# Linear attention and two MoE layers on one core: banks by kind, a head pair moved forward, Strassen's second product in the first MoE's last pair

## The chip, the cores and the metric

The kernel runs on one core of one Trainium2 chip. The metric is the device time of a whole execution in microseconds. TensorE (PE in the profile) multiplies matrices into PSUM, whose eight banks hold 512 fp32 values per partition each; its weight loads are listed as PEld. VectorE (DVE) and ScalarE (ACT) do elementwise work, SyncE (SP) issues every DMA.

## The reference

```python
kv = np.einsum('bhsd,bhse->bhde', k, v)            # 8 batches, 8 heads, 576 positions, 64 wide
out = np.einsum('bhsd,bhde->bhse', q, kv)
x = out / np.sqrt(np.mean(out * out, -1, keepdims=True) + 1e-06) * g_norm   # then (4608, 512)
r = np.maximum(x @ w_in, 0.0);  x = (s * (r * r) + b) @ w_out               # first MoE, d_ff 2048
h = x @ w2_in;  out = (h * (1.0 / (1.0 + np.exp(-1.702 * h)))) @ w2_out     # second MoE, d_ff 2048
```

## The kernel before, in words

The 4608 tokens are 9 blocks (j) of 512. Every product of fp32 values is made of three matmuls in fp32r: each operand is split into a high part (ACT copies to fp32r) and a low part (DVE subtracts), and high x high, high x low and low x high are added in PSUM. The weights arrive as 64-bit words and are converted on ACT and DVE (w_low, w_top, w_sum: lines L138 to L152).

Blocks 0 to 2 of the first MoE and block 8 of the second are done plainly: `mlp_h` makes one of 16 hidden parts f (12 matmuls into one bank h, L447), `mlp_act` applies the activation and gives the bank back, `mlp_g` splits, and `mlp_o` adds 12 matmuls into the four banks of the block's output (L490). The other blocks go in pairs. `first_products` makes x @ w_in by Strassen's scheme in Winograd's form: seven products a to g for each of 8 pairs of hidden parts (L533), with sums on DVE. For the second product, the first MoE's pairs (3, 4), (5, 6), (7, 8) use `second_plain` (16 parts x 2 blocks x 12 matmuls, L490), and the second MoE's pairs use `second_products` (seven products of 4 groups of 12 matmuls, L661; `go_sum`, `go_hi`, `go_lo` make its operands, L626, L635, L640). Strassen's weight operands (A11, S1 and so on) lie in DRAM.

Attention for block j and head pair p is a row of seven steps: `att_product` (o_ps, L345), square, low, `att_mean` (ms, L373), `att_root`, `att_newton` (L387 to L389, the last reader of both banks) and `att_split`. Products k^T v (kv) of the next batches come two head pairs at a time (L316, L320); ACT copies them out (L324, L325).

All order is written out by hand. `at(slot, function, ...)` puts a step at a slot; one slot is 12 matmuls of PE. The steps are sorted by slot and then issued, so every engine and the DMA queue of SP works in that order. Tiles are taken from lists of numbered places: 43 big and 20 middle ones in SBUF and 8 PSUM banks. A place that is given back goes to the end of its list, and the next taker gets the first; a taker waits on the chip until the last reader is done.

`START` holds the slots of the four head pairs of block 0: kv product; attention product, square and low; mean and root; newton; split.

Of the kernel before, what the change touches and what calls it, by code (L numbers as in the profile page):

```python
# [26 lines left out]
START = [(-61, -60, -54, -52, -45), (-59, -54, -53, -47, -42), (-54, -48, -48, -43, -41), (-50, -49, -46, -40, -36)]  # L27
# [12 lines left out]
LAG = 2  # L40
G1_ACT = (0, 0, 0, 1.5, 0.2, 1.6, 1.6)
# [20 lines left out]
def kernel(ctx: ExitStack, tc: tile.TileContext, qT, kv_h, kvt, cst,  # L62
# [32 lines left out]

    def psum(name):
        return new(bank, [P, T], F32, name)
# [23 lines left out]
    raws, vals, W = {}, {}, {}  # L121
# [49 lines left out]
    wod = [dp.tile([P, 2, 512], F32, name=f"wod{f}") for f in range(NF)]  # L171
    wsd = [[dp.tile([P, len(OPS), 512], F32, name=f"wsd{m}_{i}") for i in range(NF // 2)] for m in range(2)]
    wo2 = [dp.tile([P, NF // 2, 512], F32, name=f"wo2{name}") for name in OPS]

    def op_place(m, i, which, name):
        return wo2[OPS.index(name)][:, i, :] if which else wsd[m][i][:, OPS.index(name), :]
# [6 lines left out]
    def wo_store(f):  # L183
        nc.sync.dma_start(out=wod[f], in_=W[0, f, 1].bitcast(F32))

    def wo_load(m, f):
        w = W[m, f, 1] = new4(F32R, "w")
        if m == 0:
            nc.sync.dma_start(out=w.bitcast(F32), in_=wod[f])
        else:  # L190
            for a, name in enumerate(OP_PAIRS[1][f % 2]):
                nc.sync.dma_start(out=w[:, a, :].bitcast(F32), in_=op_place(m, f // 2, 1, name))

    def a_store(f):
        w = W[0, f, 0]
        for c, name in enumerate(OP_PAIRS[0][f % 2]):
            nc.sync.dma_start(
                out=op_place(0, f // 2, 0, name).rearrange("p (h c) -> p h c", h=2),
                in_=w[:, :, c * 256:(c + 1) * 256].bitcast(F32),
            )  # L200

    def w_join(f):
        w = W[0, f, 0]
        q = vals[0, f, 0] = new2(U32, "ca")
        dve.tensor_add(out=q.bitcast(F32), in0=w[:, 0, :].bitcast(F32), in1=w[:, 1, :].bitcast(F32))

# [43 lines left out]
    def wi_load(m, f):  # L250
        t = W[m, f, 0] = new4(F32R, "w")
        for a, name in enumerate(OP_PAIRS[0][f % 2]):
            nc.sync.dma_start(out=t[:, a, :].bitcast(F32), in_=op_place(m, f // 2, 0, name))

    def w_part(m, f, which, h, c):
        w = W[m, f, which]
        if m == 0:
            return w[:, h, c * P:(c + 1) * P]
        return w[:, c // 2, h * 256 + c % 2 * P:h * 256 + (c % 2 + 1) * P]
# [179 lines left out]
    def mlp_h(m, j, f):  # L439
# [9 lines left out]
        if m or j == NPLAIN - 1:  # L449
            drop(W.pop((m, f, 0)))  # L450
        if f == NF - 1:
# [41 lines left out]
    def wo_done(m, f):  # L493
        drop(W.pop((m, f, 1)))

# [93 lines left out]

    def g2_scale(q, n):  # L590
# [56 lines left out]
    def go_load(k, n):  # L647
        t = wl["o", k, n] = new4(F32R, "wl")
        nc.sync.dma_start(out=t.bitcast(F32), in_=wo2[OPS.index(PRODUCTS[k][0])][:, 2 * n:2 * n + 2, :])
# [40 lines left out]
    def g2_store(j, k, d):  # L690
        n, half = {3: (1, 2), 4: (0, 0), 5: (0, 2), 6: (1, 0)}[k]
        o_store(1, j + n, half + d, so.pop(("st", k, d)))
# [31 lines left out]
    def first_products(m, base, shift):  # L724
        for i in range(NF // 2):
# [7 lines left out]
            if i % 2 and m == 0:  # L733
                for n, (q, fn) in enumerate((("22", AF.Relu), ("21", AF.Relu), ("22", AF.Square), ("21", AF.Square),
                                             ("12", AF.Relu), ("11", AF.Square), ("12", AF.Square))):
                    at(slot + 1.4 + 0.45 * n, r_act, q, i // 2, fn)
            elif i % 2:
                at(slot + 3.1, t_sums, i // 2)
        return base + 28 + shift

    def second_plain(j, base):
        for f in range(NF):
            at(base + 2 * f - LEAD, wo_load, 0, f)
# [13 lines left out]
    def second_products(j, base):  # L757
        for k in range(len(PRODUCTS)):
            for n in range(4):
                slot = base + 4 * k + n  # L760
                at(slot, g2_product, k, n)
                at(slot - LEAD, go_load, k, n)
# [3 lines left out]
            for d in range(2):  # L766
                at(slot + 0.6 + 0.5 * d, g2_sum, j, k, d)
                if k > 2:
                    at(slot + 2.6, g2_store, j, k, d)
# [212 lines left out]
```

## Time and profile before

| | us |
|---|---|
| median of 3 runs (lowest, highest) | 1580.91 (1580.14, 1582.62) |
| the profiled execution | 1580.11 |
| its span, first to last instruction | 1578.3 |
| mean granted clock of TensorE | 0.998 |

A profile lists every instruction of one execution with its engine, start and length. A wait of an engine is put down to the instruction whose semaphore came last. "h <- DVE y L389" reads: the product h was waiting for the DVE operation of line 389. The granted clock is the share of 2.4 GHz; 0.5 is 1.2 GHz.

### The profile page before, as it was taken

The numbers are of one execution on the slowest core, as the hardware profiler recorded it, in microseconds if no ns is written. First come the engines' busy times: TensorE is split into PE (matmuls) and PEld (weight loads), VectorE is DVE, ScalarE is ACT, GpSimd is POOL, SyncE is SP. The second block draws the span as 40 slices with busy tenths as digits, with TensorE's granted clock in tenths as the row PEclk, the third lists the DMA queues.
The fourth block names the chain that finished last, engine by engine and source line by source line (L and its number), as shares of the span: only waits on it lengthen the run. The fifth ranks groups of instructions, "written<-read, shape, count | busy, mean of one in ns | idle before, by whom it ended". The sixth has DMA issues, their size and how long they took to land.

```text
span 1578.3 us, 19674 instructions
## 1 busy us (share of the span) xinstructions
PE 1552.8 (98%) x6904; PEld 1274.9 (81%) x6904; DVE 1095.9 (69%) x1583; ACT 861.0 (55%) x1283; POOL 2.4 (0%) x12
## 2 busy tenths in 40 slices
PE   7998999999999999999999999999999999999999
PEld 5777888788788877888888888888888888888887
DVE  5987356776789578856672679777967896688422
ACT  5987566655898379944783225423532452334222
POOL 0000000000000000000000000000000000000000
PEclk9999999999999999999999999999999999999999
DMA  9863646658987798859970866885788577745780
GB/s 323 250 204 113 233 138 230 224 189 308 341 278 280 243 377 277 306 181 358 333 295 0 301 239 236 273 299 200 269 284 303 200 250 262 263 149 205 230 296 27
DMA packets 171298, 385.36 MB, mean 244 GB/s; under 512 B 21312, under 2 KB 56768, under 8 KB 171200
## 3 DMA queue, kind: packets, MB, share of 16 engines
q1 hardware_dynamic: 171200, 384.11, 70.1%
q8 instruction: 55, 0.90, 0.2%
q14 instruction: 43, 0.35, 0.1%
HBM read 292.95 MB, written 91.10 MB: 243 GB/s over the span
## 4 chain that ended last, share of the span: by engine, by line
PE 76%; ACT 2%; DVE 2%; DMA 1%; issue 1%; DVEq 0%; ACTq 0%
PE o L490 21%; PE o L661 19%; PE d L533 9%; PE a L533 9%; PE h L447 4%; PE b L533 4%; PE f L533 4%; PE c L533 4%; ACT r L588 1%; DMA wsd<-op 1%; PE o_ps L345 0%; PE ms L373 0%; DMA wl<-wsd 0%; DVE y L387 0%; DVE y L388 0%
## 5 line engine op out<-in xcount | busy, mean ns | idle before, releaser
L490 PE MATMUL o<-gh,w 128*128 128x512 f32 x1280 | 409.7, 393 | 0.2
L490 PEld LDWEIGHTS o<-gh,w 128*128 128x128 f32 x1280 | 240.9, 188 | 52.0 <-DVE w L167 0.8
L661 PE MATMUL o<-gh,wl 128*128 128x512 f32 x896 | 276.7, 389 | 0.0
L490 PE MATMUL o<-gl,w 128*128 128x512 f32 x640 | 250.1, 391 | 0.3 <-DVE gl L480 0.2
L661 PEld LDWEIGHTS o<-gh,wl 128*128 128x128 f32 x896 | 168.3, 188 | 34.8
L447 PE MATMUL h<-xh,w 128*128 128x512 f32 x512 | 174.6, 403 | 8.8 <-DVE y L389 4.9
L661 PE MATMUL o<-gl,wl 128*128 128x512 f32 x448 | 174.5, 389 | 0.0
L533 PE MATMUL d<-xh,wl 128*128 128x512 f32 x448 | 157.5, 392 | 0.2
L533 PE MATMUL a<-xh,wl 128*128 128x512 f32 x448 | 157.7, 393 | 0.0
L490 PEld LDWEIGHTS o<-gl,w 128*128 128x128 f32 x640 | 120.7, 189 | 27.2 <-DVE gl L480 1.3
L447 PEld LDWEIGHTS h<-xh,w 128*128 128x128 f32 x512 | 96.9, 189 | 32.5 <-issue 5.6
L549 ACT ACTIVATE c<-a 128x512 f32<-128x512 f32 x56 | 33.3, 595 | 157.1 <-PE a L533 151.4
L447 PE MATMUL h<-xl,w 128*128 128x512 f32 x256 | 100.8, 394 | 0.4 <-DVE xl L409 0.4
L533 PEld LDWEIGHTS d<-xh,wl 128*128 128x128 f32 x448 | 84.2, 188 | 18.5 <-DVE r L559 1.0
L533 PEld LDWEIGHTS a<-xh,wl 128*128 128x128 f32 x448 | 84.1, 188 | 17.8 <-issue 0.2
L661 PEld LDWEIGHTS o<-gl,wl 128*128 128x128 f32 x448 | 84.1, 188 | 17.4
L604 DVE TENSOR_TENSOR gl<-r,gh 128x512 fp32r<-128x512 f32 x96 | 65.2, 687 | 46.4 <-ACT gh L599 45.0
L635 ACT ACTIVATE gh<-t 128x1024 fp32r<-128x1024 f32 x48 | 51.0, 1062 | 71.8 <-DVE t L626 71.6
L533 PE MATMUL a<-xl,wl 128*128 128x512 f32 x224 | 87.3, 390 | 0.0
L533 PE MATMUL d<-xl,wl 128*128 128x512 f32 x224 | 87.3, 390 | 0.0
L588 ACT ACTIVATE r<-r 128x1024 f32<-128x1024 f32 x84 | 84.9, 1047 | 0.0
L570 ACT ACTIVATE t<-a 128x512 f32<-128x512 f32 x32 | 19.1, 598 | 117.4 <-PE a L533 105.8
(118 smaller groups left out, 2719.4 us busy)
## 6 DMA issues: line engine op xcount, KB each, us to landing
wl<-wsd SPq DMA_DIRECT2D x168, 512.0 KB, 7.1
wl<-wo2S SPq DMA_DIRECT2D x64, 512.0 KB, 5.1
wsd<-op SPq DMA_DIRECT2D x96, 256.0 KB, 4.0
w<-wod SPq DMA_DIRECT2D x48, 512.0 KB, 6.1
wl<-wo2A SPq DMA_DIRECT2D x48, 512.0 KB, 3.7
raw<-in_w_in SPq DMA_DIRECT2D x32, 512.0 KB, 8.1
kv_in<-in_kv SPq DMA_DIRECT2D x32, 512.0 KB, 5.6
raw<-in_w_out SPq DMA_DIRECT2D x32, 512.0 KB, 7.6
```

Of the source, the lines that this page charges most:

```text
L447: pe.matmul(h, lhsT=a, rhs=b, start=(n == 0), stop=(n == 3 * NP - 1))
L490: pe.matmul(acc[m, j][c], lhsT=a, rhs=x, start=(f == 0 and n == 0), stop=(f == NF - 1 and n == 2))
L533: pe.matmul(o, lhsT=a, rhs=b, start=(first and n == 0), stop=(n == 5), skip_group_check=not first)
L549: act.activation(st["c1"], st[0], AF.Copy)
L570: act.activation(t, h, AF.Sigmoid, scale=1.702)
L588: act.activation(R[q, n], R[q, n], fn)
L604: dve.tensor_sub(out=gl, in0=R[q, i][:, half, :], in1=gh.bitcast(F32))
L635: act.activation(hi, src, AF.Copy)
L661: pe.matmul(so[k, d], lhsT=a, rhs=b, start=(first and n == 0 and i == 0 and e == 0), stop=(n == 3 and i == 1 and e == 2), skip_group_check ...
```

## The change

PSUM: a bank now remembers the kind of its last user. Attention's o_ps and ms are kind 1, h and kv kind 2, all others 0. A taker of kind 1 or 2 gets the first free bank that its own kind had last, if there is one, and the first of the list if not. `START` moves the third head pair forward, and the other times a little. The pair (7, 8) of the first MoE uses `second_products`; so W_out's operands of the first MoE are kept in DRAM in Strassen's form too (`part_store`, `w_rejoin`, `s_sums` and the rest during the second product of pair (3, 4)), and `part_load` reads a plain weight in two DMAs from there. That pair's activations get an order of their own. The conversions of the second MoE's weights go by a list, `CONV_AT`, of slots; before, there was one each 9.5 slots from 100, W_in and W_out in turn. The first stage of the second MoE gets its operands from `x_sums` and `x_splits`. In block 0 the even hidden parts are split as in blocks 1 and 2.

```diff
-START = [(-61, -60, -54, -52, -45), (-59, -54, -53, -47, -42), (-54, -48, -48, -43, -41), (-50, -49, -46, -40, -36)]
+START = [(-61, -60, -54, -52, -45), (-59, -54, -53, -47, -43), (-54, -51, -49, -45, -42.5), (-50, -48.9, -46, -41, -40.6)]
+SECOND = 7
+CONV_AT = ((97, 4), (156, 4), (188, 4), (221, 1), (232, 1), (250, 1), (278, 1))
...
+    last = {}
     def psum(name):
+        kind = {"o_ps": 1, "ms": 1, "h": 2, "kv": 2}.get(name, 0)
+        own = [n for n in bank.free if last.get(n) == kind]
+        if kind and own:
+            bank.free.remove(own[0])
+            bank.free.insert(0, own[0])
+        last[bank.free[0]] = kind
         return new(bank, [P, T], F32, name)
...
+    def part_load(m, f, which):
+        w = W[m, f, which] = new4(F32R, "w")
+        for a, name in enumerate(OP_PAIRS[which][f % 2]):
+            nc.sync.dma_start(out=w[:, a, :].bitcast(F32), in_=op_place(m, f // 2, which, name))
+        loaded.add((m, f, which))
...
+    def w_rejoin(f):
+        w = W[0, f, 1]
+        q = vals[0, f, 1] = new2(U32, "ca")
+        dve.tensor_add(
+            out=q.bitcast(F32).rearrange("p (a c) -> p a c", a=2),
+            in0=w[:, :, 0:256].bitcast(F32), in1=w[:, :, 256:512].bitcast(F32),
+        )
...
-        if m == 0 and j == 0:
+        if m == 0 and j == 0 and f % 2:
             act.activation(r, r, AF.Identity, scale=s_col, bias=b_col)
             act.activation(gh, r, AF.Copy)
         elif m == 0:
...
+            elif m == 0:
+                at(slot - 1.2, r_act, "11", i // 2, AF.Square)
+                at(slot - 0.7, g2_scale, "11", i // 2)
+                for n, q in enumerate(("22", "12", "21")):
+                    at(slot + 0.6 + n, r_relu2, q, i // 2)
+                    at(slot + 1.2 + n, g2_scale, q, i // 2)
+                at(slot + 3.0, t_sums, i // 2)
...
     for j in range(NPLAIN, NB, 2):
         firsts[0, j] = base
-        seconds[0, j] = first_products(0, base, LAG if j == NPLAIN else 0)
-        base = second_plain(j, seconds[0, j])
+        both = j >= SECOND
+        seconds[0, j] = first_products(0, base, LAG if j == NPLAIN else 0, both)
+        base = second_products(0, j, seconds[0, j]) if both else second_plain(j, seconds[0, j])
...
-    x_operands(1, 0, seconds[0, NB - 2] + 5, 2.3)
-    for j in range(0, NB - 3, 2):
-        x_sums(j + 2, firsts[1, j] + 4, 2)
-        x_splits(j + 2, seconds[1, j] + 5, 3.1)
+    for j, k in [(0, (0, NB - 2))] + [(j + 2, (1, j)) for j in range(0, NB - 3, 2)]:
+        x_sums(j, firsts[k] + 4 if j else seconds[0, NPLAIN] + 24, 2)
+        x_splits(j, seconds[k] + 5, 3.1)
...
+    for i in range(NF // 2):
+        slot = seconds[0, NPLAIN] + 4 * i
+        at(slot - 0.6, w_rejoin, 2 * i)
+        at(slot + 1.4, w_rejoin, 2 * i + 1)
+        at(slot + 2.2, s_sums, 0, i, 1)
+        for k in (2, 3):
+            at(slot + k + 1, op_hi, 0, i, 1, k)
+            at(slot + k + 1.7, op_lo, 0, i, 1, k)
+            at(slot + k + 4, op_store, 0, i, 1, k)
+        at(slot + 5, op_done, 0, i, 1)
```

## Rows read from the trace of the kernel before

**Rows 1.** The page: busy us, share of the span, instructions of each engine

```profile
PE 1552.8 (98%) x6904; PEld 1274.9 (81%) x6904; DVE 1095.9 (69%) x1583; ACT 861.0 (55%) x1283; POOL 2.4 (0%) x12
```

**Rows 2.** Chain that ended last: start us, length us, engine and line

```profile
791.02 87.04 PE o L490 x384
...
1106.57 76.16 PE o L661 x336
```

**Rows 3.** Waits of PE: us in total, times, longest

```profile
PE h L447 <- DVE y L389: 4.9, 1, 4.9
PE o_ps L345 <- DVE y L389: 3.1, 1, 3.1
...
PE h L447 <- ACT r L459: 1.1, 1, 1.1
```

**Rows 4.** Busy time by stage: first token block, then blocks two and three

```profile
27.00:153.70 126.70, 113.86 (x531) 90.37 (x529) 109.75 (x192) 107.86 (x193) 0.00 (x0) 0.97 0.65 204
153.70:358.60 204.90, 202.77 (x932) 167.86 (x931) 118.72 (x195) 125.27 (x201) 0.00 (x0) 1.00 0.61 206
```

**Rows 5.** Timeline of the start, by engine: DVE, PE, ACT (start, length us)

```profile
17.38 0.75 DVE L389 SCALAR_TENSOR_TENSOR y<-o_ps,g_col,y 128x512 f32<-128x512 f32 x1
...
26.97 0.58 PE L447 MATMUL h<-xh,w 128*128 128x512 f32 x1
...
32.88 0.25 ACT L324 ACTIVATE kvs<-kv 64x128 f32<-64x128 f32 x1
33.15 0.27 ACT L325 ACTIVATE kvs<-kv 64x128 f32<-64x128 f32 x1
...
38.94 0.60 ACT L459 ACTIVATE r<-h 128x512 f32<-128x512 f32 x1
...
44.76 0.59 ACT L459 ACTIVATE r<-h 128x512 f32<-128x512 f32 x1
```

**Rows 6.** Timeline of PE and ACT around a kv product of block two

```profile
165.71 1.95 PE L316 MATMUL kv<-kv_in 128*128 128x128 f32 x16
...
167.73 0.58 PE L447 MATMUL h<-xh,w 128*128 128x512 f32 x1
168.12 0.27 ACT L324 ACTIVATE kvs<-kv 64x128 f32<-64x128 f32 x1 [2.55 <-PE kv L320]
...
168.40 0.27 ACT L325 ACTIVATE kvs<-kv 64x128 f32<-64x128 f32 x1
```

**Rows 7.** Timeline at the start of the last block

```profile
1487.20 0.39 PE L447 MATMUL h<-xh,w 128*128 128x512 f32 x1
...
1490.12 0.60 ACT L462 ACTIVATE r<-h 128x512 f32<-128x512 f32 x1 [19.08 <-PE h L447]
...
1490.75 0.69 DVE L463 TENSOR_TENSOR r<-h,r 128x512 f32<-128x512 f32 x1 [2.66 <-ACT r L462]
```

**Rows 8.** Busy time in a second_products stage: PE, PEld, DVE, ACT

```profile
1117.30:1128.20 10.90, 10.90 (x50) 9.04 (x49) 10.37 (x10) 6.95 (x8) 0.00 (x0) 1.00 0.61 197
1128.20:1139.00 10.80, 10.80 (x49) 8.97 (x48) 10.80 (x11) 5.21 (x5) 0.00 (x0) 1.00 0.72 239
```

**Rows 9.** Timeline of DVE and PE in the same stage

```profile
1117.76 1.23 DVE L640 TENSOR_TENSOR gl<-r,gh 128x1024 fp32r<-128x1024 f32 x1 [1.72 <-ACT gh L635]
...
1141.90 1.21 DVE L640 TENSOR_TENSOR gl<-t,gh 128x1024 fp32r<-128x1024 f32 x1
...
1144.71 0.39 PE L661 MATMUL o<-gl,wl 128*128 128x512 f32 x1
```

**Rows 10.** DVE timeline of a weight conversion, and groups of two lines

```profile
62.37 0.42 DVE L145 TENSOR_SCALAR cu<-cu 128x512 f32<-128x512 f32 x1
...
64.63 0.68 DVE L167 TENSOR_TENSOR w<-ca,w 128x512 fp32r<-128x512 f32 x1
...
L230 DVE TENSOR_TENSOR op<-ca,op 128x512 fp32r<-128x512 f32 x32 | 21.8, 683 | 0.8 <-ACT op L225 0.8
...
L588 ACT ACTIVATE r<-r 128x1024 f32<-128x1024 f32 x84 | 84.9, 1047 | 0.0
```

**Rows 11.** Busy time and granted clock (0.83) around a stall of PE

```profile
80.00:90.00 10.00, 7.70 (x35) 6.22 (x36) 9.51 (x18) 7.21 (x13) 0.00 (x0) 0.83 0.58 196
```

More of the change, by code (lines that the diff above doesn't have):

```diff
@@ L248, in op_load @@
         nc.sync.dma_start(out=t[:, 0:n, :].bitcast(F32), in_=wsd[m][i][:, 2 * k:2 * k + n, :])
[L250 to L253, printed above, removed]
     def w_part(m, f, which, h, c):
         w = W[m, f, which]
-        if m == 0:
-            return w[:, h, c * P:(c + 1) * P]
-        return w[:, c // 2, h * 256 + c % 2 * P:h * 256 + (c % 2 + 1) * P]
+        if (m, f, which) in loaded:
+            return w[:, c // 2, h * 256 + c % 2 * P:h * 256 + (c % 2 + 1) * P]
+        return w[:, h, c * P:(c + 1) * P]
     kvin, kvs, qin, xT, done = {}, {}, {}, {}, set()
@@ L732, in first_products @@
                     at(slot - LEAD, op_load, m, i, k // 2)
-            if i % 2 and m == 0:
+            if i % 2 == 0:
+                continue
+            slot += 1.2
+            if m == 0 and not both:
                 for n, (q, fn) in enumerate((("22", AF.Relu), ("21", AF.Relu), ("22", AF.Square), ("21", AF.Square),
                                              ("12", AF.Relu), ("11", AF.Square), ("12", AF.Square))):
-                    at(slot + 1.4 + 0.45 * n, r_act, q, i // 2, fn)
-            elif i % 2:
-                at(slot + 3.1, t_sums, i // 2)
+                    at(slot + 0.2 + 0.45 * n, r_act, q, i // 2, fn)
+            elif m == 0:
[5 more added lines that the diff above has]
+                at(slot + 3.0, t_sums, i // 2)
+            else:
+                at(slot + 1.9, t_sums, i // 2)
         return base + 28 + shift
@@ L755, in second_plain, with second_products @@
         return base + 32
-    def second_products(j, base):
+    def second_products(m, j, base):
         for k in range(len(PRODUCTS)):
@@ L768, in second_products @@
                 if k > 2:
-                    at(slot + 2.6, g2_store, j, k, d)
+                    at(slot + 2.6, g2_store, m, j, k, d)
         return base + 28
@@ L915 @@
         at(slot + 4, op_done, 0, i, 0)
-    slot = 32 * NPLAIN + 4
     for i in range(NF // 2):
-        for which in range(2):
-            for n in range(2):
-                u = (1, 2 * i + n, which)
-                at(slot - 4, w_load, *u)
-                at(slot + n, w_low, *u)
-                at(slot + n + 1, w_top, *u)
-                at(slot + n + 1.5, w_sum, *u)
-            at(slot + 3.5, s_sums, 1, i, which)
-            for k in range(4):
-                at(slot + 3 + 1.2 * k, op_hi, 1, i, which, k)
-                at(slot + 4 + 1.2 * k, op_lo, 1, i, which, k)
-                at(slot + 6 + 1.2 * k, op_store, 1, i, which, k)
-            at(slot + 7.7, op_done, 1, i, which)
-            slot += 9.5
+        slot = seconds[0, NPLAIN] + 4 * i
[7 more added lines that the diff above has]
+        at(slot + 5, op_done, 0, i, 1)
+    slots = [base0 + 8 * n for base0, count in CONV_AT for n in range(count)]
+    for n, slot in enumerate(slots):
+        i, which = n % 8, n // 8
+        for n in range(2):
+            u = (1, 2 * i + n, which)
+            at(slot - 4, w_load, *u)
+            at(slot + n, w_low, *u)
+            at(slot + n + 1, w_top, *u)
+            at(slot + n + 1.5, w_sum, *u)
+        at(slot + 3.5, s_sums, 1, i, which)
+        for k in range(4):
+            at(slot + 3 + 1.2 * k, op_hi, 1, i, which, k)
+            at(slot + 4 + 1.2 * k, op_lo, 1, i, which, k)
+            at(slot + 6 + 1.2 * k, op_store, 1, i, which, k)
+        at(slot + 7.7, op_done, 1, i, which)
     for f in range(NF):
-        at(base + 2 * f - LEAD, wi_load, 1, f)
-        at(base + 2 * f + 2 * LAG - LEAD, wo_load, 1, f)
+        at(base + 2 * f - LEAD, part_load, 1, f, 0)
+        at(base + 2 * f + 2 * LAG - LEAD, part_load, 1, f, 1)
     events.sort(key=lambda e: e[:2])
```

61 lines of the change are left out of this document (28 added, 33 removed).

## The prediction

> **What bounds the kernel now.** I read the page's busy times first, then the waits of PE, the chain that ended last, a table of busy times by stage, and last the timeline around five places that the change touches. The reader is to see in the page that PE is busy 98% of the span and DVE 69% [rows 1]: as an average that leaves DVE much room, and the stages will show that it has none where it counts. The chain runs through the second products without a gap: 384 matmuls of the plain form take 87.04 us and 336 of the Strassen form 76.16 us [rows 2], 226.7 ns each, so twelve of them (one "slot" of the order) take 2.72 us. PE waits in few places [rows 3]: 4.9 and 3.1 us for the attention's last DVE operation (L389), whose bank a hidden product h or an attention product o_ps had been given, and 1.1 us for an ACT operation that reads h. All three lie in the first token block. There, from 27 to 153.7 us, PE is busy 113.86 of 126.70 us and DVE and ACT 109.75 and 107.86: three engines close to full. In the two blocks after it PE is busy 202.77 of 204.90 us [rows 4]. So PE bounds everything but the first block, and a change gains by fewer matmuls and loses by any wait that PE gets.
>
> **Part 1, Strassen in the last pair.** Second_plain for block 7 becomes second_products: 7 products x 4 x 12 = 336 matmuls for 384. **-10.9 us** (87.04 - 76.16) [rows 2], certain if nothing delays PE there.
>
> **Part 2, what DVE must do in that stage.** The same code already runs in the second MoE, so its trace is the model. From 1117.30 to 1139.00 us DVE is busy 10.37 of 10.90 and 10.80 of 10.80 us [rows 8]: in that stretch it is full, while PE is just fed. The last idle time of DVE there ends at 1117.76, when ACT delivers; the low part of the third product in the fourth group is made at 1141.90 (it lasts 1.21) and PE uses it at 1144.71: 1.6 us to spare, the least in the stage [rows 9]. The change puts one weight conversion (the lone one at slot 250, four slots into this stage; CONV_AT) with its DVE work between those two points. Its price: two weights, each from the start of L145 to the start of the next thing, 64.63 - 62.37 = 2.26 us, so 4.5; four lows of 0.68 (2.4 at the pace of back-to-back operations); four half-width sums at some 0.4 (an estimate from the 0.68 of the full width), 1.5: 8.4 us [rows 10]. DVE is in order and full, so that low part comes 8.4 us later and PE waits 8.4 - 1.6 = 6.8 us in all, spread over groups three and four. One more thing is late: in the first MoE the squares and scales of the last rows are 1024 wide (1.05 us each on ACT [rows 10]) and stand at slots 1.3 to 3.9 of the stage between the high parts; nine of them in 10.9 us with five others of ACT make the first gl some 2 to 3 us later than in the model. Bounds: 0 if DVE had the room that its 69% promises, 10.4 with ACT's lateness in full. I take **+8.5 us**, nearer the upper end, since the rows of this very stage show a full DVE.
>
> **Part 3, the banks.** The new rule of psum() lets kind 2 (h, kv) take a free bank that kind 2 had last. Writing the free list out by hand: the warm-up takes bank 0, the first kv takes bank 1 and gives it back in the same event; the next kv finds bank 1 as its own, and so does every one after it. h is taken at slot 2f and given back at 2f + 1 (mlp_act), and kv falls at odd slots just behind that. So no h or kv ever finds its own bank busy in the order, and **all h and kv products of the plain blocks share one bank**. Each must then wait until ACT (in the last block DVE too) has read the one before. Three places pay:
>
> (a) Blocks two and three. Behind an ordinary h comes an o product of 2.72 us, and the ACT read takes 0.6 us: hidden. But h follows kv directly. The kv product starts at 165.71, h at 167.73, and ACT's two copies of kv run from 168.12 to 168.67 (168.40 + 0.27) [rows 6]: h would wait 0.95 us. Of the five such places left after the first block, three are like this and in two an attention product stands between (0.3 each): **+3.4 us**. Bounds: 3.0, and 6 if ACT is behind at each by another 0.5.
>
> (b) The last block starts with three h in a row. PE starts the first at 1487.20 and would start the second 2.72 us later, 1489.92; sigmoid (0.60 from 1490.12) and multiply (0.69 from 1490.75) have read the bank at 1491.44 [rows 7]. 1.5 us for the second, the same for the third: **+3.1 us**, with nothing beside it to hide it. Bounds 2.8 to 3.4.
>
> Rows 6 and 7 show what rotation hid. The Trainium skill says the same in general (Perfetto Trace Analysis, Optimizing Tensor Performance): independent matmul groups should rotate through different PSUM banks, so that one is emptied while the next is computed. Taken whole, it would charge all 62 changes from one h to the next 0.6 us, some 37 us, and the whole would come to 1616 us; the trace charges only those without an o product between, which is the sum here.
>
> (c) The first block. What goes: the two stalls on L389 (8.0 us) [rows 3], since attention keeps three banks of its own and an attention product takes the one free longest; and with them the half clock that follows each (0.83 granted over the 10 us around the first [rows 11], so 3.4 us at 1.2 GHz for 2.4, which loses 1.7 us; the 0.97 of the whole stage [rows 4] makes two of these). What comes: h0 now waits for the first kv's copies. Today h0 starts at 26.97, before its last operand is there, and the copies start at 32.88 and end at 33.42 (33.15 + 0.27) [rows 5]; in the new order a high part of 0.6 us stands ahead of them. START also moves the third pair's product forward, but its own bank is that of the first pair, read until 18.13 (17.38 + 0.75) [rows 5], and the fourth kv queues behind it on PE. So h0 starts at about 35. Then h1 waits for the reader of h0 (38.94, 0.60 long; now some 1.5 later) and the next kv for that of h1 (44.76) [rows 5]: about 3 us each. From h0 to h16 PE has 110 us of pure work (113.86 less the slow clock and doubled records, an estimate), plus eight times 1 us behind kv, plus 6: 35 + 124 = 159, for 153.7 today. The even f move 0.63 us of ACT to 0.55 of DVE, eight times; this stands in the noise of the estimate. Bounds: -3 (h0 at 33.5, ACT prompt) and +9 (DVE, the fuller one, gets 4.4 us more and sets the pace). I take **+4 us**.
>
> **Part 4, the rest, +1 us.** Loads and stores of W_out split in two have the same bytes and lie behind PE's 87 us stages. The sums for the new operands (8 times some 4.4 us of DVE in the first second_plain) take the place of three conversions (25 us) there, and DVE's mean of 69% [rows 1] holds the other 10; if that cover is gone, PE waits for gl, up to those 10 us. Conversions every 8 slots for 9.5 beside the attention of block 3: PE waits nowhere there now. 0 to 5, I take 1, from the empty side.
>
> **Sum.** -10.9 + 8.5 + 3.4 + 3.1 + 4 + 1 = +9.1 us. The profiled run took 1580.1 us (span 1578.3 and 1.8 around it), 0.8 below the median of the three. So 1580.9 + 9.1 = **1590.0 us**. What can be told from no change is about 0.2%, 3.2 us.
>
> **Rivals.**
> *DVE absorbs the conversion* (part 2 costs 1 instead of 8.5): 1590.0 - 7.5 = 1582.5. For it: the mean load, and that sums can run ahead while DVE waits for ACT. Against it: rows 8. It decides if DVE's idle time between 1117 and 1142 is over 7 us; it is under 1.
> *The bank rule gains* (other side): the stalls of the first block and the clock behind them go, 8.0 + 3.4 + 1.1 = 12.5 us, and h loses nothing there because ACT keeps up: part 3c becomes about -9 (3.5 go to the later h0), and with part 2 as said and (a) and (b) halved, 1580.9 - 10.9 + 8.5 + 3.2 - 9 + 1 = 1573.7. It turns at the point where ACT reads h within the 2.72 us of an o product; the rows show ACT reading h0 at 38.94, 12 us after PE began it, and h1 another 5.8 later [rows 5], with ACT 85% busy [rows 4], which speaks against it.
> *The clock falls again and again*: the new waits of 3 us and more (before h0, before kv in the first block, in group three of Strassen) each bring half speed, as the waits of 3.1 and 4.9 us do today [rows 3, 11], at 1.7 us each. Six of them: 1600. For it: the wait before h0 is over 7 us. Against: most new waits are 1 to 2 us, and the stage's 0.97 leaves no third such stretch for today's wait of 1.1 us.
> *No effect on the whole* (within 3.2 us): gains and waits cancel at 1579 to 1584; this is the first rival and the shallow end of the bounds together.
>
> **Numbers.** Forecast as summed 0.58 (its own range 1585 to 1596), clock 0.15, DVE absorbs 0.14, bank rule gains 0.10, other 0.03. Slower by over 0.2%: the forecast, the clock and a little of the third, 0.75; within: most of the third, 0.12; faster: the bank rival and a little of the third, 0.13. The range leaves out the bank rival and the far end of the clock: 1577 to 1602.
>
> **What would show it.** In the second products of block 7, waits of PE L661 on DVE L640 of 7 to 10 us together, and the group of 336 taking about 85 us, not 76. PE h L447 waiting on ACT L325 (14 times, about 1 us where ACT is prompt) and on ACT L459; in the last block two waits of 1.5 us on DVE L463. No wait on L389 by h. h0 starting after 33 us. The prediction is wrong if h still starts before the copies of kv end, if 336 matmuls take 76 us in block 7, or if the first block ends before 152 us.

## The result, and the profile after

The changed kernel takes 1603.63 us (median; 1601.89 to 1605.81) beside 1580.53 for the kernel before on the same chip: a ratio of 1.0143, interval [1.0126, 1.0159], 23.1 us slower. The direction was forecast, the size was not: 1590.0 was the forecast, and its range ended at 1602.0. Two runs, one of the kernel before (3182.9 us) and one of a kernel below (2995.32, kv given a kind of its own), took nearly twice as long as all others and are left out of the ratios and intervals.

The page's busy line of the changed kernel, as in [rows 1]:

```profile
PE 1553.6 (97%) x6856; PEld 1267.8 (79%) x6856; DVE 1166.6 (73%) x1677; ACT 877.0 (55%) x1287; POOL 2.4 (0%) x12
```

PE has 48 matmuls fewer and is no less busy; DVE has 71 us more. The span went from 1578.3 to 1603.7, so PE's new time is idle time and matmuls at half clock. (The profiled execution of the changed kernel is the longest of its four, 2.2 us above the median.) Its waits (us in total, times, longest) answer to [rows 3]:

```profile
PE h L456 <- ACT kvs L334: 13.8, 13, 7.3
PE kv L325 <- ACT r L469: 6.1, 4, 2.1
PE o L676 <- DVE gl L655: 6.0, 3, 2.4
PE d L544 <- DVE r L570: 5.0, 4, 2.0
PE h L456 <- DVE r L473: 2.8, 2, 1.4
PE h L456 <- ACT r L469: 2.7, 3, 1.1
```

No h waits on attention's last operation any more (L389 before, L398 now). Five of these six rows were not there before. To see where they cost, I set the start of each stage (its first h, first product or second product on PE) against the same matmul of the kernel before and took the difference of the stage lengths. Eight of the kernels run later are in the same table, with a name that their sections explain (the other three are described there); "before" is the stage's length there, the rest are differences to it, in us of the profiled execution.

| stage | before | changed | no rule | rule alone | conv moved | h+kv rule | kv own | slots 1 | slots 2 | slots 3 |
|---|---|---|---|---|---|---|---|---|---|---|
| start to first h | 26.97 | +9.5 | -0.5 | +6.4 | +9.5 | +6.5 | -0.2 | -0.2 | +2.1 | +0.7 |
| rest of the first block | 126.72 | +1.4 | +3.7 | +3.3 | +1.5 | +4.6 | -0.4 | +0.8 | -0.2 | +0.8 |
| blocks 2 and 3 | 204.94 | +2.8 | 0.0 | +2.9 | +2.9 | +2.9 | +0.2 | +0.1 | 0.0 | +0.1 |
| first products, j 3, 4 | 93.11 | +2.7 | +2.7 | 0.0 | +2.8 | 0.0 | 0.0 | +0.4 | +3.0 | +0.4 |
| first products, j 5, 6 | 88.89 | +2.2 | +1.3 | +0.1 | +1.3 | +0.1 | 0.0 | +4.6 | +2.4 | +2.3 |
| first products, j 7, 8 | 76.16 | +0.1 | 0.0 | 0.0 | +0.1 | 0.0 | 0.0 | +1.7 | 0.0 | +0.7 |
| second products, j 7, 8 | 87.04 | -0.9 | -1.0 | 0.0 | -9.2 | 0.0 | 0.0 | -8.7 | -9.2 | -9.2 |
| second MoE, first pair | 76.18 | +4.2 | +3.8 | 0.0 | +4.4 | 0.0 | +0.4 | +0.5 | +0.1 | 0.0 |
| last block | 91.12 | +3.4 | 0.0 | +3.4 | +3.6 | +3.4 | +3.5 | 0.0 | 0.0 | 0.0 |

(The pairs of the first MoE are named by their j. The stages left out differ by 0.2 at most. The first two rows belong together, since what is late at the first h may be made up in the rest of the block. Four executions in which everything up to there is the same, those of slots 1 to 3 and of the kernel without the rule and with the old opening, end the first block between 0.5 and 1.9 us later than before, so a difference of some 1.4 us says nothing there.)

**The opening.** PE, ACT and DVE around the first h of the changed kernel (start, length us), as in [rows 5]:

```profile
28.56 0.60 PE L329 MATMUL kv<-tails 128*128 128x256 f32 x2
36.50 0.79 PE L456 MATMUL h<-xh,w 128*128 128x512 f32 x1 [7.34 <-ACT kvs L334]
...
28.89 0.61 ACT L415 ACTIVATE xh<-y 128x512 fp32r<-128x512 f32 x1
34.85 0.63 ACT L415 ACTIVATE xh<-y 128x512 fp32r<-128x512 f32 x1 [5.34 <-DVE y L398]
35.39 0.61 ACT L174 ACTIVATE w<-ca 128x512 fp32r<-128x512 f32 x1
35.91 0.25 ACT L333 ACTIVATE kvs<-kv 64x128 f32<-64x128 f32 x1
36.18 0.27 ACT L334 ACTIVATE kvs<-kv 64x128 f32<-64x128 f32 x1
...
34.07 0.75 DVE L398 SCALAR_TENSOR_TENSOR y<-o_ps,g_col,y 128x512 f32<-128x512 f32 x1
```

The kv product is ready at 29, but its copies stand in ACT's order behind the high part of the fourth head pair, which waits 5.34 us for DVE's y. ACT is not busy then, it is held. With h on kv's bank, PE inherits that wait.

**Blocks two and three, and the last block.** PE of the changed kernel behind a kv product of block two, and the start of the last block, as in [rows 6, 7]:

```profile
178.35 0.60 PE L329 MATMUL kv<-tails 128*128 128x256 f32 x2
179.59 0.50 PE L456 MATMUL h<-xh,w 128*128 128x512 f32 x1 [0.64 <-ACT kvs L334]
...
1513.49 0.50 PE L456 MATMUL h<-xh,w 128*128 128x512 f32 x1 [1.41 <-DVE r L473]
...
1517.92 0.50 PE L456 MATMUL h<-xh,w 128*128 128x512 f32 x1 [1.41 <-DVE r L473]
```

After the start of block two, three h that follow kv directly come 0.99 us later than before, and two with an attention product between come 0.33 later. One of the 0.99 is made up at once, because a wait that the kernel before has just behind its place is gone from the changed one:

```profile
172.09 0.50 PE L373 MATMUL ms<-sl,ones 128*128 128x512 f32 x1 [1.01 <-DVE sl L365]
```

Together this is 2.6 of the 2.8 us in the table. The two places in the last block cost 3.4, so 1.7 each. Both prices are above the idle times (0.64 and 1.41): in the kernel before, h begins 0.36 us before the last matmul of kv ends (167.73 [rows 6] and 168.09), and here it can't.

**Strassen in the last pair.** Stages of the changed kernel (us, then PE, PEld, DVE, ACT, POOL busy, granted clock, DMA share, GB/s): the rest of the first block, the first products of j 3, 4, the second products of j 7, 8, the first products of the second MoE's first pair, and twelve microseconds within the second products:

```profile
36.50:164.65 128.15, 115.15 (x529) 90.14 (x529) 107.73 (x190) 101.09 (x181) 0.00 (x0) 0.97 0.58 177
...
372.40:468.25 95.85, 93.21 (x409) 75.55 (x408) 78.20 (x135) 73.72 (x113) 0.00 (x0) 1.00 0.87 305
...
809.62:895.72 86.10, 80.12 (x337) 65.03 (x336) 68.48 (x73) 48.62 (x55) 0.00 (x0) 0.96 0.82 284
895.72:976.08 80.36, 78.32 (x338) 64.05 (x336) 65.35 (x97) 30.69 (x51) 0.00 (x0) 0.98 0.76 268
...
832.00:844.00 12.00, 7.82 (x27) 6.06 (x28) 11.90 (x18) 4.80 (x7) 0.00 (x0) 0.86 0.42 141
```

The 336 matmuls take 86.10 us where the same code takes 76.16 in the second MoE: 5.98 of it is idle (86.10 - 80.12) and 3.96 is matmuls that take longer (80.12 - 76.16), at a granted clock of 0.96. In the stretch from 832 to 844 DVE is full, as [rows 8] led one to expect, and the clock is 0.86: part of it at 1.2 GHz in place of 2.4. DVE ahead of the longest wait, and PE at its end:

```profile
828.54 0.68 DVE L163 SCALAR_TENSOR_TENSOR cu<-raw,cu 128x512 uint32<-128x512 uint32 x1
829.26 0.69 DVE L164 CUSTOM_DVE_ANT_0 ca<-cu,ca 128x1024 uint16<-128x1024 uint16 x1
829.87 1.22 DVE L641 TENSOR_TENSOR t<-r 128x1024 f32<-128x1024 f32 x1
...
832.14 0.42 DVE L157 TENSOR_SCALAR cu<-cu 128x512 f32<-128x512 f32 x1
832.59 0.43 DVE L158 TENSOR_SCALAR cu<-cu 128x512 uint32<-128x512 uint32 x1
832.93 1.22 DVE L655 TENSOR_TENSOR gl<-t,gh 128x1024 fp32r<-128x1024 f32 x1
...
834.21 0.79 PE L676 MATMUL o<-gl,wl 128*128 128x512 f32 x1 [2.42 <-DVE gl L655]
```

cu and ca are the conversion of slot 250; the gl that PE needs stands behind them, and the matmul after the wait has 0.79 us for the ordinary 0.39. What this half clock cost is shown by the kernel without the bank rule, below.

**First products.** Of the seven products, k = 0 to 6, the last adds to bank d, so it has to wait until DVE has read what k = 3 left there (L570); products 4 (on bank a) and 5 (f) run in between. PE and DVE around such a place in the second MoE's first pair:

```profile
922.92 0.39 PE L544 MATMUL f<-xh,wl 128*128 128x512 f32 x1
925.35 0.50 PE L544 MATMUL d<-xh,wl 128*128 128x512 f32 x1 [2.04 <-DVE r L570]
...
920.47 1.22 DVE L443 TENSOR_TENSOR x<-x 128x1024 f32<-128x1024 f32 x1
921.61 0.68 DVE L244 TENSOR_TENSOR op<-ca,op 128x512 fp32r<-128x512 f32 x1
922.21 0.69 DVE L563 TENSOR_TENSOR u<-b,c 128x512 f32<-128x512 f32 x1
...
924.61 0.69 DVE L570 TENSOR_TENSOR r<-d,u 128x512 f32<-128x512 f32 x1
```

The conversion of slot 278 (its sums and lows, L228 to L244) and an x sum stand ahead of the chain u, u, r. This stage loses 2.04 idle and 2.14 of longer matmuls (78.32 - 76.18), granted clock 0.98.

### The profile page after: what moved, and what is told of

Read it like the earlier page. It is cut to its first block, busy times and chain, and to the rows that moved or that the text cites. A ratio compares the mean times of both kernels' runs of the same rounds, so it can differ in the third digit from the quotient of the medians.

```text
span 1603.7 us, 19886 instructions
## 1 busy us (share of the span) xinstructions
PE 1553.6 (97%) x6856; PEld 1267.8 (79%) x6856; DVE 1166.6 (73%) x1677; ACT 877.0 (55%) x1287; POOL 2.4 (0%) x12
## 4 chain that ended last, share of the span: by engine, by line
PE 73%; DVE 4%; ACT 2%; DMA 1%; issue 1%; DVEq 0%; ACTq 0%
PE o L676 22%; PE o L500 16%; PE d L544 9%; PE a L544 9%; PE h L456 4%; PE f L544 4%; PE b L544 4%; PE c L544 4%; PE o_ps L354 1%; ACT r L599 1%; DVE gl L655 1%; DVE t L641 0%; DMA wl<-wsd 0%; PE ms L382 0%; DMA wsd<-op 0%
## 5 line engine op out<-in xcount | busy, mean ns | idle before, releaser
L676 PE MATMUL o<-gh,wl 128*128 128x512 f32 x1120 | 347.6, 391 | 0.0
L500 PE MATMUL o<-gh,w 128*128 128x512 f32 x1024 | 328.8, 392 | 0.0
L676 PEld LDWEIGHTS o<-gh,wl 128*128 128x128 f32 x1120 | 211.8, 189 | 44.2
L676 PE MATMUL o<-gl,wl 128*128 128x512 f32 x560 | 219.6, 392 | 6.0 <-DVE gl L655 6.0
L500 PEld LDWEIGHTS o<-gh,w 128*128 128x128 f32 x1024 | 192.2, 188 | 41.0 <-issue 0.9
L500 PE MATMUL o<-gl,w 128*128 128x512 f32 x512 | 199.3, 389 | 0.0
L676 PEld LDWEIGHTS o<-gl,wl 128*128 128x128 f32 x560 | 105.8, 189 | 29.3 <-DVE gl L655 7.2
L500 PEld LDWEIGHTS o<-gl,w 128*128 128x128 f32 x512 | 96.1, 188 | 21.1 <-DVE cu L158 0.4
L655 DVE TENSOR_TENSOR gl<-r,gh 128x1024 fp32r<-128x1024 f32 x80 | 96.6, 1218 | 13.3 <-ACT gh L650 13.3
L650 ACT ACTIVATE gh<-r 128x1024 fp32r<-128x1024 f32 x80 | 81.8, 1050 | 0.4 <-issue 0.3
```

The lines of the kernel that those rows point to most:

```text
L500: pe.matmul(acc[m, j][c], lhsT=a, rhs=x, start=(f == 0 and n == 0), stop=(f == NF - 1 and n == 2))
L650: act.activation(hi, src, AF.Copy)
L655: dve.tensor_sub(out=lo, in0=src, in1=hi.bitcast(F32))
L676: pe.matmul(so[k, d], lhsT=a, rhs=b, start=(first and n == 0 and i == 0 and e == 0), stop=(n == 3 and i == 1 and e == 2), skip_group_check ...
```

## The experiments

Two questions: what does the bank rule cost and through which tiles, and what takes away Strassen's 10.9 us and slows the first products? The theories were: the loss in the plain blocks is h and kv on one bank; it is the opening's new slots; it is the clock. For the rest: the places of the lone conversions; ScalarE's wide squares; the denser conversions as such. The kernels were measured in three groups, each beside runs of the kernel before, whose medians were 1580.96, 1580.62 and 1580.52 us; each ratio is against the runs of its own group.

### The changed kernel without the bank rule

```diff
 def psum(name):
-    kind = {"o_ps": 1, "ms": 1, "h": 2, "kv": 2}.get(name, 0)
-    own = [n for n in bank.free if last.get(n) == kind]
...
     return new(bank, [P, T], F32, name)
```

> The changed kernel with the rule for banks taken out: the first free bank of the list again, START and all else as changed. Theory A (all h and kv share one bank): the waits of h on the kv copies and on its reader go, in blocks two and three (2.8 us), in the last block (3.4 us), and most of the 11.0 us of the first block with the half clock there; h0 starts before 30 us; 1603.6 - 15 = 1588, 1584 to 1592. Rival B (START is what makes h0 late): h0 still starts after 33 us, and the time falls by 6 to 8 us only, 1596. Rival C (conversions on DVE set the first block): no change of the first block, 1597.

Measured: 1590.01 us (1589.6 to 1590.48), ratio 1.0057 [1.0042, 1.0072]. The losses in blocks 2 and 3 and in the last block are gone, h starts at 26.45 again, and the waits on attention's y are back. What is left, 9.1 us above 1580.96, stands in the rest of the first block, the first products and the Strassen stage (column "no rule"). Its Strassen stage and its first products of the second MoE's first pair, to be set beside those of the changed kernel (809.62 and 895.72):

```profile
798.04:884.11 86.07, 78.97 (x337) 63.88 (x336) 68.49 (x73) 48.52 (x55) 0.00 (x0) 0.98 0.82 283
884.11:964.05 79.94, 76.98 (x338) 62.83 (x336) 65.16 (x97) 30.73 (x51) 0.00 (x0) 1.00 0.76 269
```

The Strassen stage has half as much half clock here (0.98 for 0.96). PE is idle 7.10 us for 5.98, and the stage takes 86.07 us for 86.10: the half clock of the changed kernel only filled time in which PE would otherwise have waited for DVE. The second stage has the same wait of 2.04 before d, no half clock behind it and a second wait of 0.92, and loses 3.8 us for 4.2.

### The kernel before with the bank rule alone

```diff
+    last = {}
     def psum(name):
+        kind = {"o_ps": 1, "ms": 1, "h": 2, "kv": 2}.get(name, 0)
...
```

> The kernel before with the rule for banks alone. Theory A: first block later by 8 to 11 us, blocks two and three by 2.8, last block by 3.4: 1580.5 + 15 = 1596, 1593 to 1599, with h waiting on the kv copies 13 or 14 times. Rival B (START): the last two alone, 1587. Rival D (the rule helps by itself, the stalls on the last attention operation of 8 us go): under 1580.

Measured: 1596.09 us (1595.81 to 1599.23), ratio 1.0099 [1.0084, 1.0115]: 15.1 us above the 1580.96 of before. The first products lose nothing here (0.0, 0.1 and 0.0). With the 9.1 of the run above, against the same 1580.96, this makes 24.2 for the 23.1 of the whole change: the two halves add up within the spread of the runs.

### The changed kernel without the rule, with the old opening

```diff
-START = [..., (-54, -51, -49, -45, -42.5), (-50, -48.9, -46, -41, -40.6)]
+START = [..., (-54, -48, -48, -43, -41), (-50, -49, -46, -40, -36)]
```

> The changed kernel without the rule for banks and with the START of before. Against the run without the rule alone it tells what START does by itself. Theory A: h0 starts where it did before (27 us), and START by itself is worth under 2 us either way once the bank rule is gone: within 2 us of that run. Rival B: 5 us or more faster than that run.

Measured: 1590.59 us (1588.78 to 1591.43), ratio 1.0059 [1.0044, 1.0074], the same as with the new opening. With banks in turn, moving the third head pair makes no difference to the time that can be told, though in the profiled executions the first block ends 3.1 us later than before with the new opening and 0.5 later with the old. From block two on it behaves as the kernel without the rule does (+2.8 and +1.8 us in the first products of j 3, 4 and j 5, 6, -1.0 in the Strassen stage, +4.2 in the second MoE's first pair). With the rule the profiled first h stands at 36.50 with the new opening (the changed kernel) and at 33.36 with the old (the rule alone); the 3.1 us between them shrink to 1.3 by the end of the first block (+11.0 and +9.7).

### The two lone conversions later

```diff
-CONV_AT = (..., (250, 1), (278, 1))
+CONV_AT = (..., (266, 1), (288, 1))
```

> The changed kernel with the last two lone weight conversions at slots 266 and 288 for 250 and 278. Theory E (the conversion at 250 fills DVE in the Strassen second product of the last pair, and that at 278 does so in the first products after it): the three waits on the low parts (6.0 us) and the two half-clock stretches go, 9.9 us to under 3, and the 4.2 us of the next stage to under 2: 1603.6 - 9 = 1594, 1591 to 1597. Rival F (the wide squares and scales on ACT make the low parts late): the waits stay, within 3 us of 1603.6.

Measured: 1596.37 us (1595.53 to 1598.43), ratio 1.0098 [1.0081, 1.0115], 7.3 us below the changed kernel's median. The Strassen stage now gains 9.2 of its 10.9 us; the wide squares and scales of ScalarE are still in it, so they and all else there cost at most 1.7. But the first products of the second MoE still lose 4.4, with the same wait ten slots later (a 1.97 before d at 945.20 for the 2.04 at 925.35): moving the unit from 278 to 288 moved the loss with it. The time lies where it was expected, but only one of its two terms does: in the Strassen stage PE's waits for gl fell from 6.0 us to 0.8 and 8.2 us came back, in the next stage nothing did. So 250 is confirmed as the cause, and 288 is no better place than 278.

### The bank rule for attention alone, and for h and kv alone

```diff
-kind = {"o_ps": 1, "ms": 1, "h": 2, "kv": 2}.get(name, 0)
+kind = {"o_ps": 1, "ms": 1}.get(name, 0)      # first kernel
+kind = {"h": 2, "kv": 2}.get(name, 0)         # second kernel
```

Both in the kernel before.

> The kernel before with the bank rule for the attention accumulators alone (o_ps and ms go back to a bank that attention last held; h and kv take banks in turn). Theory 1 (the rule costs through h and kv, whose two tiles follow each other on one bank while a copy still reads it; attention tiles have an interval of their own between two uses): 1577 to 1584, no measurable difference, and the stretch from block 2 to the end as before within 1 us. Theory 2 (any reuse of one bank costs in proportion to its uses): 1584 to 1592. Rival (keeping attention apart removes the waits of h and o_ps on VectorE's y): 1570 to 1576.

> The kernel before with the bank rule for h and kv alone (attention accumulators take banks in turn). Theory 1 (the whole loss of the rule is that h and kv share one bank): 1593 to 1599, as with the whole rule (1596); first h some 6 us late, last block 3.4 us longer, h after kv waiting about 0.6 us each in blocks two and three. Theory 2 (attention and first products together make the loss): 1583 to 1591.

Measured: attention alone 1580.55 us (1579.88 to 1581.95), ratio 1.0 [0.999, 1.0009]; h and kv alone 1597.35 (1596.17 to 1597.58), ratio 1.0104 [1.0089, 1.0119]. The whole loss of the rule is that of kind 2. The rule for attention alone gains nothing either, and it doesn't keep attention's banks apart: h takes the first of the list, which can be a bank that attention has just left, so the waits on y stay, 5.2 and 3.0 us for the 4.9 and 3.1 of [rows 3]. (In the trace the first h comes 0.9 us later, the first block ends 0.6 later, and every stage from block two on is as before within 0.1.) Waits of PE in the kernel with h and kv alone:

```profile
PE h L455 <- ACT kvs L333: 12.3, 12, 6.1
PE kv L324 <- ACT r L467: 7.7, 4, 2.8
PE h L455 <- ACT r L467: 3.6, 3, 1.7
PE h L455 <- DVE r L471: 2.8, 2, 1.4
```

### kv given a kind of its own

```diff
-kind = {"o_ps": 1, "ms": 1, "h": 2, "kv": 2}.get(name, 0)
+kind = {"o_ps": 1, "ms": 1, "h": 2, "kv": 3}.get(name, 0)
```

In the kernel before, with the rest of the rule.

> The kernel before with the whole bank rule, but kv given a kind of its own, so that h and kv no longer share one bank (h still follows h on one bank). Theory 1 (the loss of blocks one to three comes from h and kv on one bank, each waiting for the other's copy, that of the last block from h on one bank alone): blocks two and three as before within 0.5 us, the last block still 3.4 us longer with its two waits of 1.4 us, the first block 0 to 4 us longer, in all 1583 to 1590. Theory 2 (h on one bank alone is enough to make the loss of the first block, kv adds only its 0.6 us each): the first block still 6 to 11 us longer, 1590 to 1596.

Measured: 1583.28 us (1582.62 to 1583.64), ratio 1.0015 [1.0005, 1.0025]. Of the rule's 15 us some 12 are gone with this one digit; the last block keeps its 3.5, with its two idle times of 1.41. In the first block, where 0 to 4 us more were expected, the waits on y are gone, and it ends 0.6 us earlier, no more than such executions differ by. Waits of PE in this kernel:

```profile
PE h L455 <- ACT r L467: 9.3, 5, 5.0
PE h L455 <- DVE r L471: 2.8, 2, 1.4
```

The 8.0 us that PE waited for y, and the 1.1 for the reader of the h before [rows 3], have become 9.3 us of waiting for that reader. So with this assignment of banks the same time shows as another wait. It still lets h follow h on one bank; h in turn on several banks that attention never uses was not tried, so that no assignment can take these stalls out is not shown.

### Small matmuls ahead of the first h

```diff
+def filler():
+    t = psum("idle")
+    for _ in range(20):
+        pe.matmul(t[:, :P], lhsT=warm_sb[0], rhs=warm_sb[0], start=True, stop=True)
+    drop(t)
+at(-2.9, filler)
```

In the changed kernel.

> The changed kernel with 20 small matmuls on operands already in SBUF, on a bank of their own, put into TensorE's order just ahead of the first h, so that part of the idle time before it is filled. Theory 1 (the half-clock stretch from 31.7 to 41.9 us follows from TensorE's idle time before the first h): first h stays at 36.5 us or up to 1 us later, the half-clock stretch after it shrinks from 10.2 us by 3.4 to 6.8 us, and the time falls by 1 to 4 us to 1599 to 1603. Theory 2 (the stretch has another cause, such as the load of the opening's transfers or attention itself): same stretch, same time within 1 us.

Measured: 1602.85 us (1601.79 to 1605.26), ratio 1.0143 [1.0127, 1.0158], no difference to the changed kernel that can be told. PE had work from 27.6 to some 32.3, 4.63 us, and the granted clock of the stretch from 15 to 60 us is 0.85 for 0.81. In three parts, first this kernel and then the changed one:

```profile
15.00:30.00 15.00, 11.18 (x62) 7.64 (x61) 11.64 (x20) 10.14 (x19) 0.00 (x0) 1.00 1.07 353
30.00:45.00 15.00, 10.76 (x45) 8.05 (x43) 12.82 (x23) 10.03 (x19) 0.00 (x0) 0.77 0.86 291
45.00:60.00 15.00, 12.91 (x51) 10.37 (x52) 13.44 (x25) 11.96 (x22) 0.00 (x0) 0.77 0.71 204
```

```profile
15.00:30.00 15.00, 10.38 (x38) 6.12 (x38) 10.10 (x18) 9.92 (x19) 0.00 (x0) 0.89 1.07 356
30.00:45.00 15.00, 7.81 (x22) 5.74 (x23) 12.92 (x23) 8.69 (x17) 0.00 (x0) 0.66 0.87 293
45.00:60.00 15.00, 12.25 (x56) 9.76 (x55) 12.94 (x24) 12.26 (x23) 0.00 (x0) 0.89 0.57 161
```

From 30 to 45 us half clock shrinks from 10.2 us to 6.8 (worked out from 0.66 and 0.77), as theory 1 had it, but from 45 to 60 it grows from 3.4 to 6.8. What is left of the difference, 3.4 us before 30 us, ended at 21.5 in the changed kernel, ahead of the small matmuls, so it can't be their doing. Nor can the first h's start, 1.35 us earlier: the ms before it (24.45 for 25.82) already was. What brings the half clock of the opening is thus not shown. And the earlier first h gained nothing: from the fourth h on (58.00 for 57.80) this kernel stands 0.2 us later than the changed one.

What this half clock costs is better read from the four executions whose first block is the same (old opening without the rule, and slots 1 to 3 below). Their clock from 15 to 60 us is 0.92, 0.92, 0.89 and 0.96, and their first block ends at 154.19, 154.37, 155.55 and 155.14 us: the highest clock does not go with the earliest end.

### Sixteen conversions at other slots

Three kernels, each the changed kernel with banks in turn and the old opening:

```diff
-slots = [base0 + 8 * n for base0, count in CONV_AT for n in range(count)]
+slots = [100, 109.5, 119, 150, 159.5, 169, 178.5, 187, 193.5, 200, 206.5, 213, 221, 229, 237, 266]      # slots 1
+slots = [98, 107, 116, 125, 160, 170, 180, 187.5, 192.5, 197.5, 202.5, 207.5, 212.5, 221, 232, 266]     # slots 2
+slots = [100, 109.5, 119, 135, 160, 170, 180, 188, 193, 198, 203, 208, 213, 221, 232, 266]              # slots 3
```

Slots 1:

> The changed kernel with banks taken in turn as before, the old table of the opening, and the sixteen conversion units at slots 100, 109.5, 119, 150, 159.5, 169, 178.5, 187, 193.5, 200, 206.5, 213, 221, 229, 237 and 266: none stands closer than 9.5 slots to the next beside first products, none beside the plain second products of the last pair, and none inside the Strassen second product except at its end. Theory 1 (what the changed kernel loses outside the bank rule is set by where the conversion units stand, since VectorE then reads a bank late that TensorE is about to accumulate on): each first-products stage loses under 1 us against the kernel before, the Strassen stage of blocks 7 and 8 gains 9 to 11 us, span 1569 to 1577, ratio 0.993 to 0.998. Theory 2 (the loss comes with the wider elementwise work of the Strassen product on ScalarE and VectorE, wherever the conversions stand): the Strassen stage again gains 3 us or less and the time stays at 1582 to 1590, as without the rule.

Measured: 1581.85 us (1579.28 to 1584.98), ratio 1.0007 [0.9998, 1.0017]: 8.7 us better than the same kernel with the old list (1590.59), and outside what was expected. The Strassen stage gains 8.7 and the second MoE loses 0.5, as theory 1 has it. What it missed is the first products of j 7, 8 (+1.7) and above all those of j 5, 6 (+4.6): there PE waits 1.2 us each for attention's sl and for a load of kvbd, and longest for a weight load, in this row of its waits

```profile
PE c L538 <- DMA wl<-wsd: 2.5, 1, 2.5
```

in a stretch in which the transfers run without a pause. They do so in the kernel before as well, and there no load is late for PE; which transfer was in front of this one was not tried.

Slots 2 and slots 3:

> The same kernel as the one with sixteen re-spaced conversions (banks in turn, old opening), other slots: 98, 107, 116, 125, 160, 170, 180, 187.5, 192.5, 197.5, 202.5, 207.5, 212.5, 221, 232 and 266. Beside the first products of blocks 5 and 6 one unit fewer, beside the plain second products one every 5 slots, and in the first products of blocks 7 and 8 the two places at which the changed kernel lost nothing. Theory 1 (what is left to lose is where units meet the reads of bank d, and the transfers beside the first products of blocks 5 and 6): the 4.6 us and the 1.7 us that the run before lost in those two stages go, 1571 to 1577, ratio 0.994 to 0.998. Theory 2 (the conversions cost about the same wherever they stand, because VectorE and the transfer queue are full throughout): 1579 to 1585, the loss turning up in the plain second products instead.

> As the other re-spaced kernel, with slots 100, 109.5, 119, 135, 160, 170, 180, 188, 193, 198, 203, 208, 213, 221, 232 and 266: one unit goes beside the second products of blocks 3 and 4, where the operands of the output weights are built. Theory 1: 1571 to 1577 as well, up to 2 us from the other. Theory 2: 1579 to 1585.

Measured: slots 2 1578.33 us (1576.98 to 1580.4), ratio 0.9987 [0.9977, 0.9996]; slots 3 1576.32 (1575.27 to 1577.24), ratio 0.9973 [0.9963, 0.9982]. Slots 3 comes out as expected and beats both kernels, by 4.2 us and by 27.3. Slots 2 misses by 1.3 us: four units, 9 slots apart, beside the first products of j 3, 4 cost 3.0 us, with a wait of 1.83 before d, where three, 9.5 apart, cost 0.4. Stages of slots 3: the first products of j 3, 4 and of j 5, 6; the plain second products of j 5, 6; Strassen's of j 7, 8; and the first products of the second MoE's first pair:

```profile
360.12:453.64 93.52, 93.01 (x409) 75.56 (x408) 71.46 (x120) 69.34 (x106) 0.00 (x0) 1.00 0.84 295
540.87:632.08 91.21, 89.15 (x378) 69.53 (x376) 71.81 (x121) 70.38 (x108) 0.00 (x0) 1.00 0.93 333
632.08:719.12 87.04, 87.04 (x386) 72.10 (x384) 80.51 (x140) 71.84 (x107) 0.00 (x0) 1.00 0.96 330
795.93:873.77 77.84, 76.97 (x338) 62.76 (x337) 68.18 (x73) 48.99 (x55) 0.00 (x0) 1.00 0.79 266
873.77:949.92 76.15, 76.15 (x337) 63.06 (x336) 58.45 (x82) 25.48 (x43) 0.00 (x0) 1.00 0.77 288
```

The third line answers theory 2: with a unit every 5 slots DVE is busy 80.51 of 87.04 us and the transfers 0.96, and the 384 matmuls of the plain form still take 87.04. So what a conversion costs goes by what stands beside it. The first products of j 5, 6 still lose 2.3; a place for those units was not found.

## Why the prediction was wrong

| step | forecast | changed kernel | what the runs showed |
|---|---|---|---|
| part 1 and 2, Strassen and slot 250 | -10.9 + 8.5 | -0.9 | cause right; 9.9 lost for 8.5 |
| part 3a, blocks 2 and 3 | +3.4 | +2.8 | right; an old wait took in 1.0 |
| part 3b, last block | +3.1 | +3.4 | right |
| part 3c, first block | +4 | +11.0 | mis-sized |
| part 4, the rest | +1 | +9.2 | mis-sized |
| sum | +9.1 | +25.4 | |

The measured column is of the profiled executions, whose spans are 1603.7 and 1578.3; part 4's is the sum of the first products and the second MoE's first pair (2.7 + 2.2 + 0.1 + 4.2). Two terms failed, by 7.0 and 8.2 us.

**Part 3c, the first block.** The mechanism held: h0 waited for kv's copies, and the wait on L389 went. Three things were wrong in its sum, beside the step from its own 5.3 (159 for 153.7) to the +4 that it took. The first h came at 36.5, not 35: the copies also stand behind the high part of a head pair that ScalarE cannot make before DVE's y. The step "What goes: the two stalls on L389 (8.0 us) ... and with them the half clock that follows each" counted a gain that wasn't there. With kv on a bank of its own these stalls go too, 9.3 us of waiting for h's reader take their place, and the block is 0.6 us shorter. And the late start was not made up: from h0 to h16 PE's idle time is 13.0 us (128.15 - 115.15) where it was 12.8 [rows 4], in other waits, at the same clock of 0.97. My 124 us for this stretch, 110 of work and 14 of waits, were 128.15: the waits came to 13.0, and PE was busy 115.15, with half clock still in it. Of the block's 11.0 us the rule by itself makes 9.7. The rival "the bank rule gains" fell with the rule alone (15.1 us slower): its gain was to be those same stalls.

**Part 4, the rest.** I looked for new waits where gl is made and in "the attention of block 3", and found the cover in DVE's mean of 69% [rows 1]. The cover failed, above all at one instruction, the read of bank d (L570) that DVE must finish before product k = 6 in each round of first products: 5.0 us of waits, with 2.1 of half clock behind the longest. 1.4 more are a wait of attention's ms for DVE's sl (j 3, 4; 1.39, before 441.73), 0.8 one of product a for ScalarE, 9.3 together, for the 9.2. (Without the half clock the last of these stages lost 3.8 in place of 4.2, in the kernel without the rule, with 0.9 of waiting more.) DVE's share there is 78.20 of 95.85 us (j 3, 4) and 65.35 of 80.36 (second MoE), and still a unit that falls ahead of this read makes it late. What the unit at 278 would stand beside was not looked at in the forecast: it costs 4.2 us. Moving it to 288 takes the loss along, and with no unit there the loss is gone (slots 3, 0.0). The plain second products lose 0.2 at most in any kernel, and 0.0 with a unit every 5 slots, so there the cover was real.

**Part 2** came out near its size and by its cause, 9.9 us lost for 8.5. Moving the conversion gave back 8.2 of them, where the forecast charged 6.8 (8.4 less 1.6 to spare); ScalarE's lateness, charged with the other 1.7, made no wait that the profile shows, and the same run bounds it at 1.7. That the 9.9 show as 6.0 of waits and 4.0 of slower matmuls is the clock of this execution: the kernel without the rule has 7.1 and 2.8 in the same 86.1 us.

**The clock** was put as a rival of its own at 0.15, "each bring half speed, at 1.7 us each. Six of them: 1600". The trace has 27.3 us of half clock, 20.5 more than before. Most of it, 17.1 us, lies in the opening, where four executions of one and the same first block show no cost that can be told. Behind waits of 2.0 to 2.4 us, shorter than I took to matter, it made matmuls longer by 3.96 and 2.14 us in two later stages; but the same stages with less of it or none (86.07 for 86.10, 3.8 lost for 4.2) show that at most 0.4 of this reached the time. So the rival's 1.7 us each were not paid in any stage where two executions can be compared: DVE set the pace there, and slower matmuls took the place of waits.

**Part 3, the rule of rotation.** The Trainium skill (Perfetto Trace Analysis, Optimizing Tensor Performance) has independent groups rotate through banks. The trace agrees: 12 of the rule's 15 us come from two kinds of products on one bank, and go when each has its own. But outside the first block one bank charged only where no product of 2.72 us stands between, 0.99 and 1.7 us at a place for the forecast's 0.95 and 1.5, and not at all 62 changes. In the first block, where ACT reads late, it charged with an o product between as well (1.05 us before the h at 88.12, 1.81 before the kv at 96.66).

What stays open: which of the first block's waits would have to go, and in what order, for it to become shorter; no run here made it shorter by more than 0.6 us. The even f's move from ACT to DVE was not tried by itself; the kernel without the rule and with the old opening has it, and its first block ends 0.5 us later than before.

## What to carry to other kernels

A bank that two kinds of products share makes each wait for the other's reader, and that reader may itself be held in its engine's order: look up what stands ahead of the copy, not only how long it takes. A stall that disappears may come back as another wait; in a stage with three engines close to full, count it as nothing until a run shows it. The same holds for matmuls at half clock: where another engine sets the pace, they fill time in which PE would have waited, so compare two executions of the stage before giving them a price. Work that an engine is to absorb is priced by the single read that the bottleneck waits for beside it, instruction by instruction, and the same sixteen units made a difference of 14 us by their places alone (1590.59 and 1576.32).

## What the runs showed of the hardware

Half clock followed waits of PE of 2.0 to 2.5 us in some executions and not in others. In the changed kernel it followed one of 2.42 us (before the o at 834.21; 0.86 granted from 832 to 844 us) and one of 2.04 (before the d at 925.35; 0.98 over the stage). The same wait of 2.04 in the kernel without the rule (before the d at 913.74) was not followed by any (1.00 over the stage), nor one of 2.51 in slots 1 (before the c at 558.83; 1.00 from 540 to 633 us). The two waits of 1.41 in the last block were followed by none in any of the six kernels that have them.

What half clock cost was not its longer matmuls: the Strassen stage of j 7, 8 took 86.10 us at a granted clock of 0.96, and 86.07 (without the rule) and 86.12 (with the small matmuls) at 0.98.
